# Output rows of two attention problems: one matmul after another, or four column tiles added up by a column of ones

## The chip, the cores and the metric

One core of a Trainium2 chip runs the whole kernel. In the listings PE is TensorE, which multiplies matrices, DVE and ACT are VectorE and ScalarE, which do the elementwise work; SBUF and PSUM are memories on the chip, PSUM the one that the matmuls here write to; DMA engines bring the data in. The *granted clock* is the share of TensorE's full clock that the profile says was granted (1.00 is full, 0.50 half). The metric is the device time of one execution in microseconds (us). Each timed execution also leaves its span, which is the profile's length of the same execution, 1.6 to 2.1 us shorter in nearly all of them. The jobs ran on several chips; each job timed the kernel before beside its own kernels.

## The reference

Two decode attention problems, A and B, one query position each, 32 heads of 128, keys and values in a cache of 16384 positions. B looks at the last 4096 positions only.

```python
q = x @ wq                                  # x: 1 x 512, wq: 512 x 4096
scores = einsum("bhqd,bhkd->bhqk", q, k) * Dh ** -0.5
o = einsum("bhqk,bhkd->bhqd", softmax(scores), v)
y = o.reshape(1, 1, 4096) @ wo              # wo: 4096 x 512
return concatenate([y_A, y_B], axis=-1)     # 1 x 1 x 1024, bf16
```

The change concerns only the last product, one row of 4096 times wo, for A and for B.

## The kernel before

Keys and values stream through SBUF. Scores are made on VectorE with partial sums on TensorE; probabilities times values run on TensorE in four column tiles (a *column tile* is here a group of output partitions that begins at 0, 32, 64 or 96, each with its own matmuls). When the last values have been used, their buffer is filled with the two wo matrices: A in two loads of 16 rows of 32 each (a "row" j here is a 128x512 slice of wo), B in loads of 16, 8, 4, 2 and 2 rows (a *piece* is one load).

```python
pieces = [(stA, 0, J // 2), (stA, J // 2, J // 2)]      # J = 32
j0 = 0
for x in (J // 2, J // 4, J // 8, J // 16, J // 16):
    pieces.append((stB, j0, x))
    j0 += x
for i, p in enumerate(pieces):
    ld.add(None if i else "vt", lambda p=p: _load_wo(nc, cx, *p))
# ... all heads ...
_fin_rows(nc, cx, (stA, stB))
for p in pieces:
    _out(nc, cx, *p)
```

Each piece is then multiplied by its part of the attention output. The stationary operand has a single column (`oc[:, j]`), so a matmul leaves one row in PSUM. A takes 512 columns at once, and in the profile its matmuls start one after another, 0.216 us apart at full clock and 0.427 us at half; B is split into two halves of 256 columns that go to two column tiles (partitions 64 and 96).

```python
def _out(nc, cx, st, j0, n):
    J = st.wo.shape[0] // P
    if j0 == 0:
        # ... st.oc: bf16 copy of st.oc_ps (line 300)
    # ... out_ps: two PSUM banks
    w = st.DN // st.cols
    out = [cx.out_ps[r : r + 1, b, 0:w] for r, b in st.out_at]   # A: one, B: two
    for j in range(j0, j0 + n):
        for x in range(st.cols):
            cx.o(nc.tensor.matmul(                               # line 307
                out[x], lhsT=st.oc[:, j : j + 1], rhs=st.wo_t[:, j, x * w : (x + 1) * w],
                start=(j == 0), stop=(j == J - 1),
            ))
    if j0 + n == J:
        # ... cast to bf16 (line 316, and 318 on ScalarE for B's second half), store of the row
```

The softmax here doesn't subtract the row's maximum and nothing guards it: scores larger than these inputs give would overflow.

## Time and profile before

| | before |
|---|---|
| time, median of the first 3 runs | 823.63 us (823.02 to 823.72) |
| span of the profiled execution | 821.2 us |
| TensorE / VectorE busy | 37% / 73% |
| queue of the big loads, share of 16 DMA engines' span | 99.3% |
| last piece of B's wo lands | 818.16 us |
| end of TensorE's last matmuls | 818.63 us |

Two lines of the page first: busy tenths of the DMA engines in 40 equal slices, and the queue that carries the loads (packets, MB, share).

```profile
DMA  9999999999999999999999999999999999999997
...
q1 hardware_dynamic: 8212, 352.33, 99.3%
```

The loads keep the DMA engines busy from beginning to end: 99.3% of their span. The end of the chain of waits, in order of time (start, duration, what):

```profile
756.43 32.55 DMA vt<-in_B_v_cache_dram
...
789.00 29.16 DMA wo_t<-in_B_wo_dram
...
818.21 0.43 PE out_ps L307 x4
818.63 0.41 DVE rowB L316
```

What ends last is a load, then 0.43 us of matmuls, a cast and the store. The timeline of the part that the change touches (start, duration, engine, line, operation, count, and in brackets the engine's idle time before it and what ended it):

```profile
803.73 8.75 PE L307 MATMUL out_ps<-wo_t,ocA 128*1 128x512 bf16 x32 [0.25 <-DVE ocA L300]
...
813.35 1.91 PE L307 MATMUL out_ps<-wo_t,ocB 128*1 128x256 bf16 x32 [0.87 <-DVE ocB L300]
...
815.69 1.04 PE L307 MATMUL out_ps<-wo_t,ocB 128*1 128x256 bf16 x16 [0.43 <-DMA wo_t<-in_B_wo_dram]
...
816.91 1.00 PE L307 MATMUL out_ps<-wo_t,ocB 128*1 128x256 bf16 x12 [0.18 <-DMA wo_t<-in_B_wo_dram]
...
818.21 0.38 PE L307 MATMUL out_ps<-wo_t,ocB 128*1 128x256 bf16 x4 [0.29 <-DMA wo_t<-in_B_wo_dram]
```

Each of B's later groups waits a moment for its load: TensorE is ahead of the loads, though by only 0.2 to 0.4 us. The stretches of the same part show the granted TensorE clock (third number from the right; then DMA share and GB/s; the first numbers are the stretch's length and the busy time of each engine):

```profile
804.80:808.20 3.40, 3.40 (x9) 1.02 (x8) 0.00 (x0) 0.00 (x0) 0.00 (x0) 0.51 1.04 443
808.20:811.60 3.40, 3.40 (x17) 1.34 (x16) 0.00 (x0) 0.00 (x0) 0.00 (x0) 1.00 0.97 414
811.60:815.00 3.40, 2.53 (x37) 1.49 (x35) 0.78 (x2) 0.00 (x0) 0.00 (x0) 1.00 0.97 399
```

The clock is at half for 3.4 us, then full again, and full for all of B.

### The profile page before, as it was taken

The page shows a single profiled execution, that of the slowest core. Times are in us where ns is not written, and L with a number is a line of the kernel's source. Part 1 is how long each engine was busy: PE and PEld are TensorE (multiplying, and loading weights), DVE is VectorE, ACT ScalarE, POOL GpSimd, SP SyncE. Part 2 cuts the span into 40 slices and gives each one's busy share as a digit, 9 for nine tenths or more (in the row PEclk, how much of TensorE's full clock was granted, in tenths as well). Part 3 has the DMA queues.
Part 4 walks back from the last instruction along what each step waited for, and adds up shares of the span by engine and source line. Part 5 has one row for each costly group of instructions (what it writes and reads, how often), then busy time and mean ns, then how long its engine had stood idle before and what let it go on. Part 6 is the DMA issues. An engine that isn't in the chain of part 4 may idle for free.

```text
span 821.2 us, 4767 instructions
## 1 busy us (share of the span) xinstructions
PE 301.1 (37%) x2148; PEld 117.3 (14%) x2148; DVE 600.7 (73%) x146; ACT 35.1 (4%) x133; POOL 1.3 (0%) x9
## 2 busy tenths in 40 slices
PE   3433705143223415060606151423414250606076
PEld 1111202011011102020202020101101020202033
DVE  2099895997496867799196949599659677689921
ACT  0100000000010000000001000000001000000010
POOL 0000000000000000000000000000000000000000
PEclk9855668586767677675858585857666676768599
DMA  9999999999999999999999999999999999999997
GB/s 383 434 457 412 456 412 454 412 454 418 427 442 444 425 441 429 441 416 447 421 445 437 431 435 434 432 423 443 441 418 451 425 445 421 448 413 455 413 424 317
DMA packets 8235, 352.62 MB, mean 429 GB/s; under 512 B 916, under 2 KB 920, under 8 KB 1304
## 3 DMA queue, kind: packets, MB, share of 16 engines
q1 hardware_dynamic: 8212, 352.33, 99.3%
q8 instruction: 16, 0.26, 0.1%
q14 instruction: 3, 0.02, 0.0%
q10 hardware_dynamic: 4, 0.00, 0.0%
HBM read 352.32 MB, written 0.00 MB: 429 GB/s over the span
## 4 chain that ended last, share of the span: by engine, by line
DMA 61%; issue 15%; DVE 13%; PE 11%; ACT 0%; SPq 0%; DVEq 0%
DMA kt<-in_A_k_cache_dram 42%; DMA vt<-in_A_v_cache_dram 12%; PE red L190 7%; DVE kt L178 6%; DVE kt L169 4%; PE acc L231 4%; DMA vt<-in_B_v_cache_dram 4%; DMA wo_t<-in_B_wo_dram 4%; DVE sc L206 2%; ACT p_sb L212 0%; SPq L115 0%; PE out_ps L307 0%; DVE rowB L316 0%; DVEq L169 0%
## 5 line engine op out<-in xcount | busy, mean ns | idle before, releaser
L169 DVE TENSOR_TENSOR kt<-kt,qallA 128x32768 bf16<-128x32768 bf16 (+2 forms) x20 | 276.2, 13810 | 162.5 <-DMA kt<-in_A_k_cache_dram 162.5
L231 PE MATMUL acc<-vt,p_sb 128*8 128x512 bf16 (+1 forms) x1280 | 113.0, 530 | 444.4 <-ACT p_sb L212 344.4
L178 DVE TENSOR_TENSOR kt<-kt 128x16384 bf16<-128x16384 bf16 (+2 forms) x24 | 174.3, 7261 | 0.2
L190 PE MATMUL red<-kt,ident 128*128 128x512 bf16 x640 | 151.2, 396 | 54.6 <-DVE kt L178 54.6
L231 PEld LDWEIGHTS <-p_sb 128*8 128x8 bf16 (+1 forms) x1280 | 37.6, 112 | 515.7 <-ACT p_sb L212 419.8
L190 PEld LDWEIGHTS <-ident 128*128 128x128 bf16 x640 | 63.0, 101 | 142.2 <-issue 47.1
L169 DVE TENSOR_TENSOR kt<-kt,qallB 128x16384 bf16<-128x16384 bf16 x8 | 69.5, 8686 | 2.9 <-DMA kt<-in_B_k_cache_dram 2.9
L206 DVE TENSOR_REDUCE sc<-red 128x256 f32<-128x2048 f32 x20 | 45.7, 2284 | 5.6 <-PE red L190 5.6
L212 ACT ACTIVATE p_sb<-sc,offA 128x256 bf16<-128x256 f32 x32 | 16.0, 500 | 574.7 <-DVE sc L206 574.7
L245 DVE TENSOR_TENSOR acc<-acc,maskA 128x512 f32<-128x512 f32 x16 | 11.1, 694 | 21.4 <-PE acc L231 21.4
L212 ACT ACTIVATE p_sb<-sc,offB 128x128 bf16<-128x128 f32 x32 | 12.4, 388 | 161.2 <-DVE sc L206 161.2
L130 PE MATMUL q_ps<-wq_t,scr 128*128 128x512 bf16 x64 | 15.7, 407 | 6.9 <-DMA wq_t<-in_A_wq_dram 4.9
L251 DVE TENSOR_REDUCE s<-acc 128x128 f32<-128x512 f32 x24 | 16.6, 691 | 0.8
L307 PE MATMUL out_ps<-wo_t,ocA 128*1 128x512 bf16 x32 | 8.8, 443 | 0.3 <-DVE ocA L300 0.3
L245 DVE TENSOR_TENSOR acc<-acc,maskB 128x512 f32<-128x512 f32 x8 | 5.5, 692 | 4.5 <-PE acc L231 4.5
L130 PEld LDWEIGHTS <-scr 128*128 128x128 bf16 x64 | 6.5, 103 | 15.6 <-issue 8.0
L316 DVE CAST rowA<-out_ps 1x512 bf16<-1x512 f32 x1 | 0.7, 678 | 8.8 <-PE out_ps L307 8.8
L259 PE MATMUL f_ps<-s,selA 128*32 128x128 f32 x32 | 6.5, 285 | 0.0
L212 ACT ACTIVATION_READ_ACCUMULATOR p_sb<-sc,offA 128x1 f32 x32 | 6.0, 187 | 0.0
L212 ACT ACTIVATION_READ_ACCUMULATOR p_sb<-sc,offB 128x1 f32 x32 | 6.0, 186 | 0.0
L307 PE MATMUL out_ps<-wo_t,ocB 128*1 128x256 bf16 x64 | 4.3, 272 | 1.8 <-DMA wo_t<-in_B_wo_dram 0.9
L102 DVE CAST scr<-xT 128x128 bf16<-128x128 f32 (+1 forms) x6 | 2.1, 459 | 3.6 <-PE xT L94 3.5
(43 smaller groups left out, 26.4 us busy)
## 6 DMA issues: line engine op xcount, KB each, us to landing
kt<-in_B_k_cache_dram SPq DMA_DIRECT2D x8, 4096.0 KB, 32.4
vt<-in_B_v_cache_dram SPq DMA_DIRECT2D x8, 4096.0 KB, 23.8
wq_t<-in_A_wq_dram SPq DMA_DIRECT2D x1, 4096.0 KB, 12.2
wq_t<-in_B_wq_dram SPq DMA_DIRECT2D x1, 4096.0 KB
wo_t<-in_A_wo_dram SPq DMA_DIRECT2D x2, 2048.0 KB, 22.6
wo_t<-in_B_wo_dram SPq DMA_DIRECT2D x1, 2048.0 KB, 27.0
wo_t<-in_B_wo_dram SPq DMA_DIRECT2D x1, 1024.0 KB, 29.0
wo_t<-in_B_wo_dram SPq DMA_DIRECT2D x1, 512.0 KB
```

Of the source, the lines that this page charges most:

```text
L102: cx.o(nc.vector.tensor_copy(st.xb[:, :, g, :].rearrange("p c (i r) -> p r c i", r=R)[:, g, :, :], xT[:, :].rearrange("p (c o) -> p c o", ...
L130: cx.o(nc.tensor.matmul(q_ps[:, j, :], lhsT=st.xb[:, c, g, :], rhs=w[:, g, j * (512 // DH) : (j + 1) * (512 // DH), :], start=(g == 0 and ...
L169: cx.o(nc.vector.tensor_tensor(out=k, in0=k, in1=q.rearrange("p (o d) -> p o d", o=1).broadcast_to([P, b - a, DH]), op=ALU.mult,))
L178: cx.o(nc.vector.tensor_tensor(out=k[:, :, 0 : DH // 2], in0=k[:, :, 0 : DH // 2], in1=k[:, :, DH // 2 : DH], op=ALU.add,))
L190: cx.o(nc.tensor.matmul(load.red[:, k : k + n, :], lhsT=cx.ident[:, :], rhs=load.kt[:, k : k + n, b * W : (b + 1) * W], start=(b == 0), st ...
L206: cx.o(nc.vector.tensor_reduce(out=sc[:, :], in_=load.red[:, :, :], axis=AX.X, op=ALU.add))
L212: cx.o(nc.scalar.activation(out=u.p[:, :, g, :], in_=sc[:, u.k0 : u.k0 + n].rearrange("p (t e) -> p t e", e=4), func=ACT.Exp, scale=SCALE, ...
L231: cx.o(nc.tensor.matmul(u.acc[r : r + 4 * R, :], lhsT=u.p[:, t, :, :], rhs=u.load.vt[:, k : k + 4, :], start=(t < 4), stop=(t >= T - 4),))
L245: cx.o(nc.vector.tensor_tensor(out=acc, in0=acc, in1=st.mask[:, :].rearrange("p (x o) -> p x o", o=1).broadcast_to([P, 4, DH]), op=ALU.mult,))
L251: cx.o(nc.vector.tensor_reduce(out=u.s[:, :], in_=acc.rearrange("p x d -> p d x"), axis=AX.X, op=ALU.add,))
L259: cx.o(nc.tensor.matmul(cx.f_ps[st.f_at : st.f_at + 32, 0:DH], lhsT=st.sel[:, at : at + 32], rhs=u.s[:, :], start=(u.i == 0), stop=(u.i == ...
L307: cx.o(nc.tensor.matmul(out[x], lhsT=st.oc[:, j : j + 1], rhs=st.wo_t[:, j, x * w : (x + 1) * w], start=(j == 0), stop=(j == J - 1),))
```

## The change

Intent: A's output matmuls all go to one column tile, one after another. The value matmuls of the same kernel go to four: in the profile before, the four of each of their 320 groups start within 18 ns of each other, and 32 of them take 1.90 us at full clock, where A's 32 take 8.75 us, most of them at full clock. So put every fourth row into its own tile (output partitions 0, 32, 64, 96), so that four run at once, then add the four partial rows with one fp32 matmul by a column of ones. A does this for all 32 rows, B for its first 16; B's sum is placed after its next 8 rows, which gives its copy time.

```diff
+    if j0 < st.parts:
+        for i, (oc, wo) in enumerate(todo):
+            r = 32 * (i % 4)
+            cx.o(nc.tensor.matmul(
+                cx.out_ps[r : r + 1, st.bank, :], lhsT=oc, rhs=wo,
+                start=..., stop=..., skip_group_check=True,
+            ))
+        if j0 + n == st.parts:
+            cx.o(nc.vector.tensor_copy(cx.sums[:, st.bank, :], cx.out_ps[:, st.bank, :]))
+        todo = []
+    for i, (oc, wo) in enumerate(todo):
         for x in range(st.cols):
             cx.o(nc.tensor.matmul(
-                out[x], lhsT=st.oc[:, j : j + 1], rhs=st.wo_t[:, j, x * w : (x + 1) * w],
+                out[x], lhsT=oc, rhs=wo[:, x * w : (x + 1) * w],
                 ...
             ))
+    if j0 + n == st.sum_at:
+        for x in range(st.cols):
+            cx.o(nc.tensor.matmul(
+                out[x], lhsT=cx.ones_col[:, 0:1], rhs=cx.sums[:, st.bank, x * w : (x + 1) * w],
+                start=(j0 < st.parts), stop=(j0 < st.parts), skip_group_check=True,
+            ))
 # ... in the setup of a problem:
+        st.bank, st.parts, st.sum_at = (0, 32, 32) if name == "A" else (1, 16, 24)
 # ... before the last values are used:
+    cx.out_ps = cx.red_pool.tile([P, 4, 512], F32, tag="red", name="out_ps")
+    cx.sums = cx.kt_pool.tile([P, 2, 512], F32, tag="kt", name="sums")
+    cx.o(nc.vector.memset(cx.out_ps[:, 0:2, :], 0.0))
```

Cut: `todo` is the list of a piece's pairs of a column of the attention output (`oc`) and a row of wo; both bf16 copies of the attention output now stand together right after the placing matmuls, and the output rows moved to other PSUM banks. In the new kernel's line numbers, 307 is a tile matmul, 312 the copy of the partial rows, 322 the sum, 316 B's later rows, 328 the cast.

## The prediction

> **What bounds the kernel now.** Memory traffic. In the page's 40 slices the DMA row is 9 in all but the last (7); the queue table gives queue 1 99.3% of the 16 engines' span, 352.33 MB. TensorE is busy 37%, VectorE 73%. The chain of waits ends so: last B value load 756.43 to 788.99, last piece of B's wo (issued 789.00, landed 818.16), four matmuls 0.43 us, the row cast 0.41 us, then the store of the row to the end at 821.2.

> **The part that changes** (timeline from 803 us). A's 32 one-column matmuls run 803.73 to 812.48 (427 ns apart in 804.8:808.2, whose granted clock is 0.51; later about 213). The rowA cast takes 0.68, the ocB cast 0.17, then B's first 16 rows take 1.91 us (813.35 to 815.26). TensorE then *waits for DMA* before each of B's later pieces: 0.43 us until 815.69, 0.18 until 816.91, 0.29 until 818.21. So B's matmuls are already ahead of the loads.

> **Removed.** The value matmuls of this kernel, also four column tiles of 512 columns, took 1.90 us for 32 at full clock and four per 0.427 us at half clock, 59 or 107 ns each instead of 213 or 427. A's 32 should cost 1.9 to 3.4 us instead of 8.75; B's first 16 about 0.9 (or 1.7) instead of 1.91. [...]

> **But** A's second half of wo lands about 22.6 us after its issue at 785.7, near 808.3 (before, TensorE came just later); now TensorE will wait. B's first piece lands near 813.2 (27.0 us after 786.2); another wait. So most of the roughly 6 us gained become idle time, not an earlier end. The loads, issued 785.35 to 789.3, wait for A's value matmuls, untouched; no load moves.

> **Added.** A memset of 128x1024 fp32 (two 128x512 ones took 1.03 us) at 794.7, in DVE idle time; two 128x512 casts, about 0.7 us each; fp32 column-of-ones matmuls (A: 512 columns; B: 2 x 256), estimated at 0.4 to 1.7 us a group from the fp32 128-column ones at 273 to 285 ns. B's sum is placed after the 8-row piece, so it must fit into the waits before the 4-row piece: tight.

> **The risk.** TensorE idles more between 805 and 813 us. [...] At full clock the tail after the last landing stays 0.43 us. At half clock I estimate 1.7 (8 rows) + 0.85 (sum) + 1.7 (last 8 rows) from 815.7: the end comes about 1.3 us later.

> **Prediction.** 823.9 us, 822.8 to 825.3. Chances: faster by over 2% 0.01, within 2% 0.98, slower 0.01.

> **What would show it.** The last wo piece still lands near 818 us; A's matmuls shrink to two bursts with a DMA wait of about 3 us between them; a new wait of 1 to 4 us before B's first rows; the chain still ends with B's wo load, or, with a cold clock, with a longer run of TensorE work.

> **What would make it wrong.** [...] unprofiled runs where TensorE, not the load, ends last (then up to 1 us faster).

823.9 us lies between the time before (823.63 us) and the case of the half clock, 1.3 us later. Expecting the half clock was the author's assumption.

## The result

| | before | changed |
|---|---|---|
| time, median (first job) | 823.33 us, 4 runs | 824.35 us, 4 runs (823.47 to 825.13) |
| ratio | | 1.0012, 95% interval 0.9995 to 1.003 |
| span of the profiled execution | 821.2 us | 821.6 us |
| busy time of A's 32 output matmuls | 8.8 us | 3.8 us |

A ratio is the mean time of one kernel's fast runs over that of the other's of the same rounds, so it is not quite the ratio of the medians quoted.

The same queue line, and the end of the chain, of the changed kernel's profile:

```profile
q1 hardware_dynamic: 8212, 352.33, 99.2%
```

```profile
756.84 32.46 DMA vt<-in_B_v_cache_dram
...
789.32 29.22 DMA wo_t<-in_B_wo_dram
...
818.59 0.43 PE out_ps L316 x4
819.01 0.41 DVE rowB L328
```

It is the same chain, 0.4 us later throughout: the shift is there at 756 us already (756.84 against 756.43), long before any changed instruction, and this chain's first long key load ends 0.36 us later (42.32 against 41.96 us). So this profile shows no effect of the change on the end. The timeline shows where the saving went:

```profile
805.12 1.87 PE L307 MATMUL out_ps<-wo_t,ocA 128*1 128x512 bf16 x16 [0.25 <-DVE ocA L295]
...
808.74 1.88 PE L307 MATMUL out_ps<-wo_t,ocA 128*1 128x512 bf16 x16 [1.75 <-DMA wo_t<-in_A_wo_dram]
...
810.67 0.69 DVE L312 COPY sums<-out_ps 128x512 f32<-128x512 f32 x1 [5.51 <-PE out_ps L307]
...
811.41 1.86 PE L322 MATMUL out_ps<-sums,ones_col 128*1 128x512 f32 x2 [0.80 <-DVE sums L312]
...
813.62 1.57 PE L307 MATMUL out_ps<-wo_t,ocB 128*1 128x512 bf16 x16 [0.34 <-DMA wo_t<-in_B_wo_dram]
...
816.12 1.04 PE L316 MATMUL out_ps<-wo_t,ocB 128*1 128x256 bf16 x16 [0.94 <-DMA wo_t<-in_B_wo_dram]
...
816.99 0.60 PE L322 MATMUL out_ps<-sums,ones_col 128*1 128x256 f32 x4
...
817.42 0.91 PE L316 MATMUL out_ps<-wo_t,ocB 128*1 128x256 bf16 x12
...
818.59 0.38 PE L316 MATMUL out_ps<-wo_t,ocB 128*1 128x256 bf16 x4 [0.26 <-DMA wo_t<-in_B_wo_dram]
```

A's rows are done in two short bursts with a wait for wo between them; the sum fills most of what is left before B's first piece lands at about 813.6; the last four matmuls wait for the last piece as before. And the clock, in the same stretches as above:

```profile
804.80:808.20 3.40, 1.94 (x21) 0.51 (x17) 0.29 (x2) 0.00 (x0) 0.00 (x0) 0.50 0.97 414
808.20:811.60 3.40, 2.06 (x17) 0.46 (x17) 0.69 (x1) 0.00 (x0) 0.00 (x0) 0.50 1.01 431
811.60:815.00 3.40, 3.06 (x18) 0.50 (x16) 0.68 (x1) 0.00 (x0) 0.00 (x0) 0.54 0.95 393
```

It stays at half until about 814.7 us, where it was full from about 808.1 us before. The fall itself is not the change's doing in this profile: it comes at 804.5 us here and at 804.7 before. Here the full clock was back just in time for B's later rows.

But the profiled execution is one of four, the first, and it was the shortest. The spans of the others were 822.4, 823.1 and 822.8 us. That, and not the profile, is what had to be explained.

### The profile page after: what moved, and what is told of

It reads as the page before. It is cut to its first block, busy times and chain, and to the rows that moved or that the text cites. A ratio compares the mean times of both kernels' runs of the same rounds, so it can differ in the third digit from the quotient of the medians.

```text
span 821.6 us, 4750 instructions
## 1 busy us (share of the span) xinstructions
PE 297.5 (36%) x2138; PEld 114.5 (14%) x2138; DVE 603.0 (73%) x149; ACT 35.1 (4%) x133; POOL 1.3 (0%) x9
## 3 DMA queue, kind: packets, MB, share of 16 engines
q1 hardware_dynamic: 8212, 352.33, 99.2%
## 4 chain that ended last, share of the span: by engine, by line
DMA 61%; issue 15%; DVE 13%; PE 11%; ACT 0%; SPq 0%; DVEq 0%
DMA kt<-in_A_k_cache_dram 42%; DMA vt<-in_A_v_cache_dram 12%; PE red L190 7%; DVE kt L178 6%; DVE kt L169 4%; PE acc L231 4%; DMA vt<-in_B_v_cache_dram 4%; DMA wo_t<-in_B_wo_dram 4%; DVE sc L206 2%; ACT p_sb L212 0%; SPq L115 0%; PE out_ps L316 0%; DVE rowB L328 0%; DVEq L169 0%
## 5 line engine op out<-in xcount | busy, mean ns | idle before, releaser
L130 PEld LDWEIGHTS <-scr 128*128 128x128 bf16 x64 | 6.9, 109 | 17.1 <-issue 11.6
L307 PE MATMUL out_ps<-wo_t,ocA 128*1 128x512 bf16 x32 | 3.8, 620 | 2.0 <-DMA wo_t<-in_A_wo_dram 1.8
```

Source lines behind the costliest of these rows:

```text
L130: cx.o(nc.tensor.matmul(q_ps[:, j, :], lhsT=st.xb[:, c, g, :], rhs=w[:, g, j * (512 // DH) : (j + 1) * (512 // DH), :], start=(g == 0 and ...
L307: cx.o(nc.tensor.matmul(cx.out_ps[r : r + 1, st.bank, :], lhsT=oc, rhs=wo, start=(j0 == 0 and i < 4), stop=(j0 + n == st.parts and i >= le ...
```

## The experiments

Three readings were to be told apart.

- **Slack**: the loads of wo end last in both kernels; TensorE time saved is idle time gained, nothing more. Then the ratio is 1.
- **H, half clock**: the gaps keep the clock at half until B's rows, which in most executions then end after the last load.
- **S, sums**: the copies and the sums, set among B's matmuls, cost the microsecond whatever the clock. A further rival, C, was a difference between chips.

### Is the difference there?

`e1_after_again`: the changed kernel unaltered.

```diff
-import math
+import math  # the changed kernel again
```

> The changed kernel once more, against the kernel before, in five rounds, to see whether the 0.1% by which its first runs were longer is there. Theory (the loads of wo end last in both kernels, the matmul time saved is slack): ratio within 0.999 to 1.001. Rival (the half clock that the gaps bring lengthens the tail in executions that were not profiled): 1.001 to 1.002, again 0.8 to 1.6 us longer.

Measured: ratio 1.0015 (1.0003 to 1.0028), medians 824.56 against 823.08 us. Spans: 821.3 for the profiled run, then 822.9, 822.6, 822.9, 822.7; nine spans of the kernel before in the same job: 821.2 to 821.4. So the difference is there, small as it is, and pure slack doesn't explain it. The profiled run was again a short one and again had the clock at half, this time from about 808.5 to 815.3 us.

### How much could any faster form of A's rows save?

`e2_before_two_rows_of_a`: the kernel before, but with 2 of A's 32 output matmuls (wrong result).

```diff
-    for j in range(j0, j0 + n):
+    rows = range(j0, j0 + n) if st.cols == 2 else [j for j in (0, J - 1) if j0 <= j < j0 + n]
+    for j in rows:
```

> The kernel before with 2 of A's 32 output matmuls (wrong result on purpose): the most that any faster form of A's rows could save. Theory (slack): within 0.3 us of before, although 8 us of matmuls are gone; the last piece of wo still lands near 818 us. Rival (A's rows are on the path, and what the tiles save is lost again in casts and sums): 4 to 8 us faster.

Measured: ratio 1.0008 (0.9993 to 1.0023); spans 821.3, 822.0, 822.2, 822.2 us. Deleting 8 us of matmuls saves nothing, so A's rows were slack. But the expectation (within 0.3 us) was missed: three of the four spans are 0.6 us or more above every one of the nine before. With *less* work and no sums at all, the kernel ended later. The chain of its profile says how:

```profile
785.51 27.69 DMA wo_t<-in_B_wo_dram
...
813.24 5.46 PE out_ps L308 x58
```

The chain now ends in 5.46 us of TensorE work after B's first piece instead of in the last load. TensorE had stood idle for 4.28 us before it, and the granted clock was at half from about 806.6 to 816.9 us. This is the first direct sign of H, in a kernel without a single column tile in its output.

### Take the loads away, and the saving shows

`e3_before_small_wo` and `e4_after_small_wo`: both kernels load 2 rows of each wo and use them again and again (wrong results), so that no load of wo ends last.

```diff
-    cx.o(nc.sync.dma_start(out=st.wo_t[:, j0 : j0 + n, :], in_=src[:, j0 : j0 + n, :]))
+    if j0 == 0:
+        cx.o(nc.sync.dma_start(out=st.wo_t[:, 0:2, :], in_=src[:, 0:2, :]))
 # ... and wo_t[:, j % 2] in place of wo_t[:, j] in the matmuls
```

> The kernel before with 2 of each 32 rows of wo loaded and used again and again (wrong result on purpose), so that no load of wo can end last. Theory: matmuls start as before at about 803.7, run without a wait for a load, and end near 817.4; the time is about 1 us (0.5 to 1.6) shorter than before, no more, since TensorE was close behind. Rival (loads of wo do not bound the end): no change.

> The changed kernel with the same small loads of wo (wrong result on purpose). Theory: the gain of the tiles, hidden in the real kernel, now shows: 2 to 5 us shorter than the kernel before with small loads, less what the two sums cost (0.69 us cast and 0.6 to 1.9 us matmuls each). Rival (sums, casts and half clock eat up the whole gain): within 0.5 us of the kernel before with small loads.

Measured: 0.9974 (0.996 to 0.9988) for the first, 0.9946 (0.9933 to 0.996) for the second. Medians 821.14 and 818.73 us; spans 820.1, 818.5, 818.3, 820.2 against 815.9, 816.2, 817.9, 817.8. The mean spans, 819.3 and 817.0, differ by 2.3 us, and each kernel shows two levels about 1.8 us apart. The first gained more than the 0.5 to 1.6 us that I expected in two of its four executions; the profiled one gained 1.1 us (821.2 to 820.1).

The ends of their chains, the kernel before with small loads first:

```profile
806.05 7.08 PE out_ps L308 x32
...
813.15 0.68 DVE rowA L317
...
813.98 3.70 PE out_ps L308 x64
```

```profile
805.70 1.93 PE out_ps L308 x32
...
807.65 0.70 DVE sums L313
...
811.09 1.04 PE out_ps L317 x16
812.12 0.43 PE out_ps L323 x4
812.55 0.92 PE out_ps L317 x16
```

From the first output matmul to the last, 11.6 us (806.05 to 817.68) became 7.8 us (805.70 to 813.47), at full clock in both. So the change does what it was meant to do: in these two executions it shortens the chain of TensorE work by about 4 us, copies and sums included. (The mean spans differ by only 2.3 us: the profiled execution was of the longer level in the first kernel and of the shorter in the second.) With real loads the saving lies before the landing of the last piece.

### Is it the clock or the sums?

`e7_after_filled`: the changed kernel with 22 idle matmuls in its gaps; the result stays right.

```diff
+def _fill(nc, cx, n):
+    for i in range(n):
+        cx.o(nc.tensor.matmul(
+            cx.f_ps[0:1, :], lhsT=cx.ident[:, 0:1], rhs=cx.wo_t[:, 0, 0, :], start=True, stop=True, ...
+        ))
 # 10 after A's first half, 4 after each copy of partial rows, 4 ahead of B's rows
```

> The changed kernel with 22 idle matmuls (128x512, one column, into a free bank, never read) put where TensorE waits: 10 after A's first half, 4 after each group of tiles, 4 before B's rows. Results stay right. Theory H (in most executions the gaps leave the clock at half when B's rows come, which ends the span near 822.7 instead of 821.3): with the gaps filled every span is 821.2 to 821.6, as before, although TensorE does more work; time 823.0 to 823.3. Rival S (the copies and sums, put between B's matmuls, cost the microsecond): spans stay at 822.4 to 823.1 in most executions.

Measured: ratio 0.9998 (0.9986 to 1.0011). Spans 821.3, 821.5, 821.4, 821.7, 821.4: all five short. More TensorE work, all the copies and sums still there, and the long executions are gone. Two of the stretches used above, in its profile:

```profile
808.20:811.60 3.40, 3.40 (x30) 1.20 (x25) 0.00 (x0) 0.00 (x0) 0.00 (x0) 0.86 1.00 429
811.60:815.00 3.40, 3.40 (x27) 1.08 (x26) 1.37 (x2) 0.00 (x0) 0.00 (x0) 1.00 0.96 398
```

The full clock is back at about 809.1 us, where the unfilled kernel's profile had half until 814.7. S by itself is out, unless this chip was a different one (settled below).

`e8_tiles_in_b_alone` and `e9_tiles_in_a_alone`: each half of the change by itself.

```diff
-st.bank, st.parts, st.sum_at = (0, 32, 32) if name == "A" else (1, 16, 24)
+st.bank, st.parts, st.sum_at = (0, 0, 0) if name == "A" else (1, 16, 24)      # e8
+st.bank, st.parts, st.sum_at = (0, 32, 32) if name == "A" else (1, 0, 0)      # e9
```

> Half of the change: A's 32 rows as before (one after the other, no sum), B's first 16 rows in four column tiles with their sum. Theory H (A's short rows make the gaps, the gaps halve the clock): TensorE is busy from 804 to 813 us as before, the clock is full for B, spans 821.2 to 821.5 in every execution. Rival S (B's sum does it): spans 822.4 to 823.1 in most.

> The other half: A's rows in column tiles with their sum, B's rows as before, without a sum. Theory H: gaps as in the changed kernel, so where the clock stays at half, B's 32 rows (64 matmuls of 256 columns in pairs, 0.21 us a pair) need 6.8 us from 813.2, and spans are 822 to 823 in most executions. Rival S (B's sum does it): spans 821.2 to 821.6 in every execution.

Measured: e8 0.9999 (0.9986 to 1.0011), spans 821.3, 821.3, 821.3, 821.4, 821.7; e9 0.9999 (0.9985 to 1.0013), spans 821.4 to 821.6. The first is as H said: B's copy and sum are harmless when A's long run of matmuls precedes them. The second is a miss. A's tiles make the same gaps, and its profile has the clock at half from about 804.3 to 814.6 us like the changed kernel's; yet no execution was long. H in its first form (A's gaps alone are enough) falls; in these runs it took both halves. The timeline of this profile has 48 of B's matmuls in one unbroken run of 3.54 us from 813.45 us, where the changed kernel has a burst of tiles, then 0.80 to 0.94 us of waiting. The refined reading, H2: B's untiled rows keep TensorE busy without a break, and that brings the full clock back while the last loads still run; B's tiles, with the pause after them, do so only in some executions. This rests on the timed spans: in the two profiles themselves the clock came back at nearly the same time (814.5 and 814.7 us).

### A profile of a long execution

All profiles of the changed kernel happened to be short. `e10_after_begun_later` moves the work in time: a memset of the first loaded tile holds the first load back (0.80 to 3.09 us in the profiles, so 2.29 us, more than the 1.8 I reckoned).

```diff
         cx.wq_t = cx.vt_pool.tile([P, 2, KC, N], BF16, tag="vt", name="wq_t")
+        cx.o(nc.vector.memset(cx.wq_t[:, 0, 0, :], 0.0))
```

> The changed kernel with its first load held back about 1.8 us by a memset of the tile it fills. All profiled executions so far changed the TensorE clock at about the same times from the start of the span (808.2 and 815.0 us, 3.4 us apart); later work meets those times at another place. Theory H: B's rows now begin near 815.1, and if the stretch up to the next change does not bring back the full clock, this profile shows at last what the longer executions do: B's last 16 rows at half clock (0.21 us a pair), the last matmul 1 to 1.5 us after the last load of wo, and a chain that ends in TensorE work instead of that load. If the full clock is back in time, the span is only the 1.8 us longer, 823.1 to 823.4. Rival S: the chain ends in TensorE work with the clock at full.

Measured: one execution (state unknown for a single run), 827.37 us, span 825.5. The clock changes did not keep to the times from the start of the span that I had assumed (e2's profile, with 806.6 and 816.9, had already differed): they came at about 809.6 and 823.3 us. But the profile is the one I was after. Its chain:

```profile
788.26 27.48 DMA wo_t<-in_B_wo_dram
...
815.77 1.91 PE out_ps L308 x16
...
817.70 0.70 DVE sums L313
...
818.45 1.87 PE out_ps L317 x16
820.32 0.85 PE out_ps L323 x4
821.17 1.75 PE out_ps L317 x16
```

From the landing of B's *first* piece on, the chain is all TensorE and its copy. That copy is in it because B's next 8 rows began only after it (in e1's profile too: 0.80 us idle, ended by the copy); placing the sum after them did not hide it. The same sixteen matmuls that took 1.04 us in the short profile take 1.87 us, the sum 0.85 us of the chain instead of the 0.43 of e4. The last piece of wo landed near 820.6 us (an estimate: last issue at about 791.4, 29.2 us to landing; the two siblings below show 820.53 and 820.60), and the matmuls went on until 822.92 us.

Why did the clock not come back? I laid stretches of 3.4 us back from the moment of return, since the times between changes in these profiles are close to multiples of that. First the last three such stretches at half clock of this profile (second number: TensorE's busy time), then the one of the changed kernel's own profile that ended in the return:

```profile
813.10:816.50 3.40, 2.59 (x10) 0.45 (x14) 1.10 (x2) 0.00 (x0) 0.00 (x0) 0.50 0.98 408
816.50:819.90 3.40, 2.60 (x28) 1.11 (x22) 0.69 (x1) 0.00 (x0) 0.00 (x0) 0.50 0.62 247
819.90:823.30 3.40, 2.98 (x24) 1.32 (x20) 0.39 (x1) 0.36 (x1) 0.00 (x0) 0.51 0.01 5
```

```profile
811.30:814.65 3.35, 2.90 (x14) 0.59 (x18) 0.74 (x2) 0.00 (x0) 0.00 (x0) 0.50 0.99 411
```

Stretches with 2.59 and 2.60 us of work did not bring the clock back; those with 2.90 and 2.98 did.

The falls lie on the same grid: in the 14 traces (from 30 us on) all 301 stretches at full clock with under 1.43 us of work were followed by half clock, and none of the 791 with over 1.69 us. In e10 the clock fell at about 809.6 us although TensorE had worked until 808.06 us; the stretch before the fall had 1.31 us of work.

On this grid the profiles of the two kernels show what the change did to the clock. Before, the stretch from 804.70 us has 3.41 us of work, and the full clock is back at the next grid line, 808.11. In the changed kernel the stretches from 804.50, 807.91 and 811.32 us have 2.17, 1.88 and 2.99: two are too short of work, and the full clock is back only at 814.74. In e7 the stretch from 805.71 us has 3.03 again, and the full clock is back at 809.12.

Where the grid lies against the work differs between executions (A's first output matmul comes 0.50, 0.62 and 0.85 us after a grid line in the three profiles of the changed kernel, all short), so which part of the work falls into which stretch differs too, and that fits the two levels of the spans. In the unaltered kernel no long execution was profiled, so for it this last step is an inference from the e10 profile and from the timed runs.

### Controls

One last job on one chip: the changed kernel again, and three siblings of e10.

```diff
-import math
+import math  # the changed kernel, third time                     # e14
 # e12, e13, e11: the memset of e10 in the kernel before, in e7, in e9
+        cx.o(nc.vector.memset(cx.wq_t[:, 0, 0, :], 0.0))
```

> The changed kernel unaltered, timed on this job's chip beside the three kernels below. Theory H2 (with both groups of tiles, TensorE is too seldom busy between 805 and 817 us for the full clock to come back in time, in most executions): most spans 822.4 to 823.1, some 821.3 to 821.6, as twice before. Rival C (the earlier jobs differed by chip, not by kernel): all spans 821.2 to 821.7, as the kernel before.

> Control for the run of the changed kernel that began later (span 825.5): the kernel before with the same memset ahead of its first load, which put the first load back by 2.29 us. Theory H2: TensorE is busy throughout, nothing but the 2.3 us is added, spans 823.5 to 823.8 in every execution. Rival D (holding back the first load costs another 1.8 us of its own): 825.5.

> The changed kernel with the idle matmuls in its gaps and the later first load. Theory H2: the full clock is there when B's rows come, spans 823.5 to 823.9, 1.6 to 2.0 us less than the 825.5 of the changed kernel that began later, although TensorE has 22 matmuls more. Rival S (copies and sums): 825 or more.

> Column tiles for A's rows alone, B's rows as before, later first load. This half alone showed no longer executions, against what H said. Refined H2: B's 64 untiled matmuls keep TensorE busy without a break from its first piece on, so the full clock comes back by about 820 us, while the last loads still run; the end is at most 0.3 to 0.5 us later: spans 823.5 to 824.2. First form of H: 825 or more in this profile, as in the changed kernel.

| run | ratio to before | spans, us |
|---|---|---|
| e14, changed | 1.0007 (0.9994 to 1.0021) | 821.4, 821.2, 823.0, 823.3, 821.2 |
| e12, before, later | 1.0028 (1.0015 to 1.0042) | 824.3, 823.8, 823.9, 823.5 |
| e13, filled, later | 1.0025 (1.0011 to 1.0039) | 823.6, 823.8, 823.6, 823.5 |
| e11, tiles in A alone, later | 1.0028 (1.0014 to 1.0041) | 823.7, 823.8, 824.1, 823.7 |
| before, same job, 9 runs | | 821.4 to 821.6 (one 821.3) |

- e14 shows the two levels inside one job on one chip: three spans of 821.2 to 821.4, two of 823.0 and 823.3. Rival C (chips) falls. The split varies: 4 of 5 long in e1, 2 of 5 here.
- e13 and e11 are 1.8 to 1.9 us shorter than e10 in the profiled run, on another chip than e10 but with the same delay. With the gaps filled, or B untiled, what e10 suffered is absent in all eight executions; but e10 itself is a single one. For e11 the first form of H said 825 or more; refined H2 said 823.5 to 824.2, and that holds. Its profile had the full clock back at about 817 us, though, so the worst placement was not tested, and H2 is supported rather than shown.
- e12 is a partial miss: 823.5 to 823.8 was expected in every execution, and the profiled one had 824.3. Rival D (the delay itself costs 1.8 us more) falls with 823.5 to 823.9 in the others. The profile shows the reason:

```profile
808.71 8.42 PE out_ps L308 x32
...
817.98 3.70 PE out_ps L308 x64
```

There the value matmuls of B had run at half clock, so A's rows began 5 us later than in the unshifted profile (808.71 against 803.73, of which 2.3 are the delay), and TensorE ended the span even in the kernel before. Its slack is small, too.

Altogether the changed kernel has 14 spans: five of 821.2 to 821.6 us and nine of 822.4 to 823.3 us (means 821.3 and 822.9). The kernel before has 28, all from 821.2 to 821.6 (mean 821.4). The difference of all means is 822.31 - 821.36 = 0.95 us, 0.1%. All three profiled executions of the changed kernel were short, against 2 of the 11 others; each stands first in the list of its runs. Whether a first execution differs from later ones was not tested (e12's first was its longest).

No experiment points to a version that beats both: e7 and e8 equal the kernel before, and the end is tied to the last load, which none of them moves.

## Why the prediction was right

The number was an easy one to hit: the change touches about the last 16 of 823 us, and the range of 822.8 to 825.3 holds the time before as well. What the runs test is the mechanism.

- *Loads bound the end; the saved matmul time becomes idle time.* Right. In the short executions the chain ends with the same load and the same 0.43 us of matmuls; e2 shows that 8 us of A's matmuls can go without gain, e3 and e4 that the TensorE work is really saved (about 4 us in the profiled executions, 2.3 us in the mean spans).
- *No load moves.* Right: the wo loads began at 785.47 against 785.35 us and took 29.22 against 29.16 us.
- *A's 32 rows take 1.9 to 3.4 us.* Near: 3.75 us in two bursts at half clock (2.90 in e1), each with the tail of its last matmul. In e3 and e4, both at full clock, 7.08 us became 1.93, a factor of 3.7. The way out of PSUM got no shorter: the copy of A's four partial rows took 0.69 us, the cast of its one row before 0.68.
- *The sums cost 0.4 to 1.7 us a group.* Near, with A's just above the range: 1.86 us for A at half clock, 0.60 us for B at full clock, 1.07 us in e10. In e13, at full clock, A's sum took 1.02 us, against 0.38 us for one bf16 matmul of 512 columns in the kernel before.
- *The waits.* Two sizes were off. Between A's halves I wrote about 3 us and the profile shows 1.75, since A began 1.4 us later (B's value matmuls had met the half clock). Before B's first rows I wrote 1 to 4 us; it is 0.34, since A's sum at half clock took up most of that gap.
- *The risk of the half clock, 1.3 us later.* Right in size, and more common than I weighed it: nine of 14 executions, on average 1.5 us longer than the other five. My centre of 823.9 us was about midway between the two cases; the first median was 824.35. The trigger that I had named was not shown. From A's first output matmul on, the longest wait of TensorE was 1.75 us in the first profile and 1.51 us in e1's. In the first profile the clock was at half already when A's rows began, as in the kernel before (1.52 and 1.68 us of work in the grid stretch ahead); in e1 it fell after A's first half (1.33 us). What the change did in all of them was to leave too little work to bring it back soon.
- *What would make it wrong*: I named executions where TensorE ends last, and said the change would then be faster. The sign was wrong for the placements that the unshifted runs showed. In the later-start runs something of the kind may be seen (824.3 for the profiled e12 against 823.6 for e13), but one execution does not settle it.

## What to carry to other kernels

Before shortening work on an engine, ask what it waits for next: here each group of output matmuls was right behind its load, so 32 matmuls that took 3.75 us instead of 8.75 only waited longer. And a shorter burst may cost: in these traces TensorE's clock depended on how busy it had been (about 2.6 of 3.41 us were needed to bring it back), so taking work off it ahead of the last, unhidden matmuls made those slower: the same sixteen took 1.87 us in e10, and 1.04 us in e13 with the gaps filled. The changed kernel saves about 4 us of TensorE work (the profiles of e3 and e4) and is 0.95 us longer in the mean of its spans. When a profile shows no loss but the timed runs do, look at the spans of all executions; a profile is one draw, and here it drew the short case three times out of three.
